# Retention attention in chunks of 64 tokens on quarters of TensorE's array, in a fused attention and feed-forward kernel

## The chip, the cores and the metric

The kernel runs on one core of a Trainium2 chip. The metric is the device time of one execution in microseconds (us). Before the change, three runs took 1265.42, 1265.68 and 1266.92 us; the median is 1265.68 us. The engines are named as the profile names them: PE is TensorE's multiplying, PEld its loading of weights (the stationary operand), DVE is VectorE, ACT is ScalarE, POOL is GpSimd and SP is SyncE, whose queue issues most of the DMAs.

## The reference

Two blocks follow each other. The first is a retention attention over 8 batches, 8 heads, 576 tokens and a head size of 64; the second is a gated feed-forward network on the 4608 tokens by 512 features that the first one gives.

```python
# q, k, v: (8, 8, 576, 64) float32
scores = q @ k.transpose(0, 1, 3, 2) / np.sqrt(64)
gamma = 1.0 - 2.0 ** (-5.0 - np.arange(8))
rel = pos[:, None] - pos[None, :]
Dmat = np.where(rel >= 0, gamma[:, None, None] ** rel, 0.0)
x = (scores * Dmat) @ v                  # then (B, H, S, D) -> (B*S, H*D)

xn = x / sqrt(mean(x * x, -1) + 1e-6) * rms_g
out = (silu(xn @ w_gate) * (xn @ w_val)) @ w_out     # 512 -> 1536 -> 512
```

There is no softmax, so the attention can be cut into chunks of tokens. Within a chunk the scores are taken directly, masked and multiplied by `v`. What comes from earlier chunks is a running 64x64 state per head (the sum of decayed `k` times `v`), which is multiplied by `q`. The decay is split into factors on `v`, on the state and on the output.

## The kernel before

**Jobs and slots.** The attention is cut into 32 jobs: one job is one batch and one pair of heads. The two heads of a pair lie on partitions 0 to 63 and 64 to 127 of `qT` and `kT`. The sequence of 576 tokens is cut into four chunks of 128 and a tail of 64. `slot(j)` issues the TensorE work of two neighbouring jobs: for job j the products `scores` (L242: 8 of 64 rows by 128 columns by 128, and 2 of 64x64 for the tail) and `states` (L252: 8 products with 128 rows and 64 columns); for job j-1 the products `values` (L292: masked scores times `v`, 8 with 128 rows, 64 columns and 128 moved elements, and 2 for the tail) and `carried` (L306: state times `q`, 4 products on the whole array, with the two heads' states on the diagonal of a 128x128 tile `sd`, whose other two quarters are zero). Every float32 product shows in the trace as two records, each with its own weight load.

**DVE and ACT around it.** `weigh(j)` multiplies all four full chunks' scores by the mask in one instruction of 128x1024 (L264), then the tail (L269), and then sums the states up in a chain of one copy (L272) and three steps (L274). ACT copies the sums into the diagonal of `sd` (L280). After `carried`, three DVE instructions of 128x192 (L315) write the attention's output into `x`. `following(j)` then transposes `q` and `k` of the next job on DVE (L212), scales `v` in place on ACT (L221, L222) and issues the loads of the job after that on SP's queue.

**Feed-forward.** The tokens go in 12 blocks u of 384. Blocks 0 and 1 use plain products (L470) while the weights are still being loaded and converted. From block 2 on, `up(u, m, g)` forms seven products x, y, z, x again, w, z again, w again (L413), each of eight records of 128x192, and ACT and DVE combine them between (L437, L420, L430). `down(u, s)` (L484) multiplies by `w_out`.

**Order.** The order of all instructions is written out by hand, and each engine does its own in that order. `SLOTS` puts the slots of the attention between the products of the feed-forward: behind `up` products 0, 2, 4 and 5 of one block, behind the first `down` of the next block, and behind products 1, 3 and 5 of the third. `scores` and `states` of a job go to three PSUM banks of their own (`s`). The other five banks are a pool, from which `values` takes two and each `up` takes four.

## Time and profile before

| | us |
|---|---|
| median of 3 runs | 1265.68 (1265.42 to 1266.92) |
| the profiled execution's own time | 1266.15 |
| its span, first to last instruction | 1264.4 |
| PE busy | 1217.4 |
| PEld busy | 924.2 |
| DVE busy | 547.6 |
| ACT busy | 280.3 |
| POOL busy | 43.0 |

The span is what the profile covers; 1.75 us of the execution lie around it. A PE record's duration covers its way through the array, so records overlap, and the pace of PE is read from the distance of their starts, not from their durations. The mean granted clock of TensorE was 0.984. In a row of the timeline stand the start and the duration in us, then engine, line, operation, out<-in and shape, the count of instructions (x) and in brackets the idle time before and who ended it.

### The profile page before, as it was taken

What the parts mean: (1) busy time and instruction counts of PE and PEld (TensorE: products, weight loads), DVE (VectorE), ACT (ScalarE), POOL (GpSimd) and SP (SyncE); (2) the same over time, 40 slices, a digit from 0 to 9 for tenths busy, and PEclk for the clock granted to TensorE, in tenths of its full rate; (3) what the DMA queues carried; (4) which work ended last, traced back from release to release, by engine and by line L of the source; (5) the groups of instructions that cost most, each with busy time, mean ns of one, the idle gap of its engine ahead of it and who ended that gap; (6) DMA issues with size and microseconds to landing.
All of it is one profiled execution on the core that took longest, in us unless ns stands there. A gap on an engine that the chain in (4) does not pass through costs nothing.

```text
span 1264.4 us, 16414 instructions
## 1 busy us (share of the span) xinstructions
PE 1217.4 (96%) x6792; PEld 924.2 (73%) x6792; DVE 547.6 (43%) x1056; ACT 280.3 (22%) x520; POOL 43.0 (3%) x44
## 2 busy tenths in 40 slices
PE   4599799999999999999999999999999999999998
PEld 3465455447976985976985995995995896795993
DVE  1789871015542652433552464343454443333240
ACT  3646541011221220111120221121221121120110
POOL 0000005130000000000000000000000000000000
PEclk8899799999999999999999999999999999999999
DMA  8579520022230322002122233002122200000000
GB/s 212 123 177 198 141 100 0 17 62 45 46 74 17 68 51 54 1 9 54 38 40 58 38 59 68 9 1 53 27 57 53 45 1 10 17 1 17 9 1 25
DMA packets 225307, 65.68 MB, mean 52 GB/s; under 512 B 212688, under 2 KB 212816, under 8 KB 225232
## 3 DMA queue, kind: packets, MB, share of 16 engines
q1 hardware_dynamic: 215872, 45.12, 17.3%
q10 hardware_dynamic: 9360, 19.51, 4.7%
q8 instruction: 53, 0.87, 0.3%
q14 instruction: 22, 0.18, 0.0%
HBM read 55.16 MB, written 9.44 MB: 51 GB/s over the span
## 4 chain that ended last, share of the span: by engine, by line
PE 88%; DVE 5%; ACT 3%; DMA 2%; issue 1%; SPq 1%; POOL 0%; DVEq 0%; ACTq 0%; POOLq 0%
PE out L484 29%; PE x L413 12%; PE w L413 12%; PE z L413 12%; PE y L413 6%; PE up L470 6%; PE s L242 3%; PE av L292 2%; PE av L306 2%; PE s L252 1%; DMA k<-in_k_dram 1%; ACT w_gate L548 1%; PE ms L360 1%; DVE w_gate L572 1%; DMA v<-in_v_dram 1%
## 5 line engine op out<-in xcount | busy, mean ns | idle before, releaser
L484 PE MATMUL out<-w_out,h 128*128 128x512 f32 x792 | 346.1, 594 | 0.0
L484 PEld LDWEIGHTS out<-w_out,h 128*128 128x128 f32 x792 | 149.1, 190 | 177.5 <-issue 175.1
L489 ACT COPY o_all<-out 128x512 f32<-128x512 f32 x36 | 21.1, 586 | 348.8 <-PE out L484 334.9
L420 DVE TENSOR_TENSOR u<-m,y 128x384 f32<-128x384 f32 x60 | 33.2, 554 | 149.9 <-PE y L413 141.8
L264 DVE TENSOR_TENSOR ret<-s,causal 128x1024 f32<-128x1024 f32 x32 | 39.2, 1224 | 121.8 <-PE av L292 69.3
L413 PE MATMUL x<-x,w_gate 128*128 128x192 f32 x480 | 88.9, 328 | 1.5 <-ACT m L437 1.5
L413 PE MATMUL x<-x,w_val 128*128 128x192 f32 x480 | 89.2, 329 | 0.0
L413 PE MATMUL w<-sums,w_gate 128*128 128x192 f32 x480 | 87.8, 326 | 0.0
L413 PE MATMUL w<-sums,w_val 128*128 128x192 f32 x480 | 87.8, 326 | 0.0
L413 PE MATMUL z<-x,w_gate 128*128 128x192 f32 x480 | 87.8, 326 | 0.0
L413 PE MATMUL z<-x,w_val 128*128 128x192 f32 x480 | 87.8, 326 | 0.0
L413 PEld LDWEIGHTS x<-x,w_gate 128*128 128x128 f32 x480 | 79.2, 190 | 7.1 <-issue 4.3
L413 PEld LDWEIGHTS x<-x,w_val 128*128 128x128 f32 x480 | 78.8, 190 | 1.4 <-ACT m L437 1.4
L413 PEld LDWEIGHTS w<-sums,w_gate 128*128 128x128 f32 x480 | 79.7, 190 | 0.0
L413 PEld LDWEIGHTS z<-x,w_val 128*128 128x128 f32 x480 | 79.7, 190 | 0.0
L413 PEld LDWEIGHTS z<-x,w_gate 128*128 128x128 f32 x480 | 79.7, 190 | 0.0
L413 PEld LDWEIGHTS w<-sums,w_val 128*128 128x128 f32 x480 | 79.7, 190 | 0.0
L280 ACT ACTIVATE sd<-sum,gc 64x256 f32<-64x256 f32 x64 | 32.3, 504 | 200.4 <-DVE sum L274 200.0
L470 PE MATMUL up<-x,w_gate 128*128 128x384 f32 x192 | 67.8, 515 | 1.5 <-ACT w_gate L548 0.8
L420 DVE TENSOR_TENSOR h<-u,w 128x384 f32<-128x384 f32 x60 | 33.3, 555 | 81.4 <-PE w L413 81.4
L432 ACT ACTIVATE h<-h 128x384 f32<-128x384 f32 x90 | 47.0, 523 | 88.6 <-DVE h L420 88.6
L382 DVE SCALAR_TENSOR_TENSOR x<-x,rms_g,rb 128x384 f32<-128x384 f32 x48 | 26.3, 608 | 89.1 <-PE rb L380 89.1
(98 smaller groups left out, 1345.7 us busy)
## 6 DMA issues: line engine op xcount, KB each, us to landing
out_dram<-o_all SPq DMA_DIRECT2D x36, 256.0 KB, 2.0
k<-in_k_dram SPq DMA_DIRECT2D x64, 128.0 KB, 2.8
v<-in_v_dram SPq DMA_DIRECT2D x64, 128.0 KB, 2.8
qraw<-in_q_dram SPq DMA_DIRECT2D x112, 72.0 KB, 2.4
kraw<-in_k_dram SPq DMA_DIRECT2D x112, 72.0 KB, 2.6
w_out<-in_moe_w_gate_dram ACTq DMA_DIRECT2D x6, 1024.0 KB, 6.6
w_out<-in_moe_w_val_dram ACTq DMA_DIRECT2D x3, 1024.0 KB, 5.9
w_gate<-in_moe_w_val_dram ACTq DMA_DIRECT2D x3, 1024.0 KB, 6.2
```

Of the source, the lines that this page charges most:

```text
L242: nc.tensor.matmul(s[:, e, ck] if c < NFULL else s[e * n : e * n + n, 2, :n], lhsT=d["kT"][r, ck], rhs=d["qT"][r, ck], start=True, stop=True,)
L264: nc.vector.tensor_tensor(out=ret.rearrange("p e (c k) -> p e c k", c=NFULL), in0=s[:, :2].rearrange("p e (c k) -> p e c k", c=NFULL), in1 ...
L280: nc.scalar.activation(out=sd[j % 2][r, :, r], in_=t[r], func=AF.Copy, scale=gc[r, hp : hp + 1])
L292: nc.tensor.matmul(av[blk][e * D : e * D + D, o : o + n], lhsT=d["v"][:, c, e] if c < NFULL else d["vt"][r], rhs=d["ret"][:, e, c * P : c ...
L306: nc.tensor.matmul(av[blk][:, o : o + n], lhsT=sd[j % 2][:, c - 1], rhs=d["qT"][:, c * P : c * P + n], start=False, stop=(c in (AC - 1, NC ...
L382: nc.vector.scalar_tensor_tensor(out=x[:, c], in0=x[:, c], scalar=rms_g[:, c : c + 1], in1=rb[:, :U], op0=ALU.mult, op1=ALU.mult,)
L413: nc.tensor.matmul(ps[:, i * HU : i * HU + HU], lhsT=w_up[m][:, 2 * blk + c, cut], rhs=t_of[u][blk][:, c], start=(start and i == c == 0), ...
L420: nc.vector.tensor_tensor(out=o, in0=a, in1=pairs_of(ps), op=ALU.add)
L432: nc.scalar.activation(out=o, in_=c, func=AF.Silu)
L470: nc.tensor.matmul(ps[:, :U], lhsT=w_up[m][:, 4 * half + c, i * P : i * P + P], rhs=x_of[u][:, c], start=(c == 0), stop=(c == NHP - 1),)
L484: nc.tensor.matmul(ps[:, :DM], lhsT=h_of[u][:, f, s * P : s * P + P], rhs=w_out[:, f], start=(f == 0), stop=(f == NF - 1),)
L489: nc.scalar.copy(out=o, in_=ps[:, :DM])
```

## The change

The chunk becomes 64 tokens: nine chunks (`NC`), numbered in pairs (`i, odd = divmod(c, 2)`). All attention products become 64x64x64, each on one quarter of the array: rows 0 to 63 or 64 to 127 by columns 0 to 63 or 64 to 127. `scores` takes rows by head and columns by the chunk's parity, `states` and `values` take rows by parity and columns by head, `carried` takes rows and columns by head, which are the two quarters on the diagonal. A tenth pair of scores repeats chunk 8, so that DVE has a full shape to read.

`sd` and its copies by ACT go; `carried` reads the sums directly, and the sums are kept in two buffers. The sum is a chain over eight chunks. The mask is one instruction for each head, which also multiplies by a constant. The state of chunk 7 finds no room in `s` and takes a bank `last` of the pool of five. The output is written by four instructions that step over every second chunk. `vt` (the tail of `v`) is loaded by one DMA instead of two and scaled by two instructions instead of one. Two small tables are no longer loaded, and another one is smaller.

In `slot`, `values` of the job before now comes ahead of `scores` and `states`. Behind the last product of `values`, GpSimd writes one element (`tick`) once that product is done, and the first product of `carried` waits for that write.

```diff
 def load_kv(j):
...
-        t = st[j]["vt"] = raw.tile([P, D], F32, tag="vt", name=f"vt_{j}", bufs=3)
-        for e in range(2):
-            nc.sync.dma_start(
-                out=t[e * TAIL : e * TAIL + TAIL], in_=v[b, 2 * hp + e, NFULL * P :]
-            )
+        t = st[j]["vt"] = raw.tile([L, 2, D], F32, tag="vt", name=f"vt_{j}", bufs=3)
+        nc.sync.dma_start(
+            out=t, in_=v[b, 2 * hp : 2 * hp + 2, NFULL * P :].rearrange("e p d -> p e d")
+        )
...
 def scale_v(j):
...
-            t = d["v"][:, :, e]
-            nc.scalar.activation(out=t, in_=t, func=AF.Copy, scale=gv[:, hp, e : e + 1])
-        nc.scalar.activation(out=d["vt"], in_=d["vt"], func=AF.Copy, scale=gt[:, hp : hp + 1])
+            for t in (d["v"][:, :, e], d["vt"][:, e]):
+                nc.scalar.activation(
+                    out=t, in_=t, func=AF.Copy, scale=gv[: t.shape[0], hp, e : e + 1]
+                )
+    def side(i):
+        return slice(i * L, i * L + L)
 def scores(j):
...
+        for c in range(NC + 1):
+            i, odd = divmod(c, 2)
+            c = min(c, NC - 1)
             for e in range(2):
                 nc.tensor.matmul(
+                    s[side(odd), e, i * L : i * L + L], lhsT=d["kT"][side(e), c * L : c * L + L],
+                    rhs=d["qT"][side(e), c * L : c * L + L], start=True, stop=True,
                 )
+    def state_of(d, c):
+        i, odd = divmod(c, 2)
+        if odd and SC + i * L == 512:
+            return d["last"][:, :L]
+        return d["s"][:, 1, SC + i * L : SC + i * L + L] if odd else d["s"][:, 2, i * L : i * L + L]
 def states(j):
...
+        d["last"] = bank(f"last_{j}")
+        for c in range(NC - 1):
+            i, odd = divmod(c, 2)
+            o = state_of(d, c)
+            for e in range(2):
+                nc.tensor.matmul(
+                    o[side(e)], lhsT=d["k"][side(odd), i, e],
+                    rhs=d["v"][side(odd), i, e], start=True, stop=True,
                 )
 def weigh(j):
...
+        ret = d["ret"] = att.tile([P, 2, NFULL + 1, L], F32, tag="ret", name=f"ret_{j}", bufs=1)
+        for e in range(2):
             nc.vector.scalar_tensor_tensor(
+                out=ret[:, e], in0=s[:, e, :SC].rearrange("p (c k) -> p c k", k=L),
+                scalar=float(_gamma(H)[2 * hp + e] ** -L),
+                in1=causal.unsqueeze(1).to_broadcast([P, NFULL + 1, L]),
+                op0=ALU.mult, op1=ALU.mult,
+            )
+        t = d["sum"] = att.tile([P, NC - 1, L], F32, tag="sum", name=f"sum_{j}")
+        for c in range(NC - 1):
+            part = state_of(d, c)
+            if c == 0:
+                nc.vector.tensor_copy(out=t[:, 0], in_=part)
+                continue
+            nc.vector.scalar_tensor_tensor(
+                out=t[:, c], in0=t[:, c - 1], scalar=gc[:, hp : hp + 1], in1=part,
                 op0=ALU.mult, op1=ALU.add,
             )
-        for e in range(2):
-            r = slice(e * D, e * D + D)
-            nc.scalar.activation(
-                out=sd[j % 2][r, :, r], in_=t[r], func=AF.Copy, scale=gc[r, hp : hp + 1]
-            )
+    def follow(a, b):
+        why = mybir.DependencyInfo(mybir.DependencyClass.Sync, mybir.DependencyReason.DATA)
+        tc.add_manual_dep(a.ins, b.ins.name, why, reason="rows of the array")
 def values(j):
...
+            i, odd = divmod(c, 2)
             for e in range(2):
+                mm = nc.tensor.matmul(
+                    av[odd][side(e), i * L : i * L + L],
+                    lhsT=d["v"][side(odd), i, e] if c < NC - 1 else d["vt"][:, e],
+                    rhs=d["ret"][side(odd), e, i],
+                    start=(c < 2), stop=False, skip_group_check=True,
+                )
+        d["valued"] = nc.gpsimd.memset(tick, 0.0)
+        follow(d["valued"], mm)
 def carried(j):
...
+            for e in range(2):
+                mm = nc.tensor.matmul(
+                    av[odd][side(e), i * L : i * L + L], lhsT=d["sum"][side(e), c - 1],
+                    rhs=d["qT"][side(e), c * L : c * L + L],
+                    start=False, stop=(c >= NC - 2), skip_group_check=True,
+                )
+                if c == 1 and e == 0:
+                    follow(mm, d["valued"])
...
+            for first in (c0 // L, c0 // L + 1):
+                i, odd = divmod(first, 2)
+                n = -(-(c1 // L - first) // 2)
                 nc.vector.tensor_tensor(
+                    out=x[:, first - c0 // L :: 2],
+                    in0=av[odd][:, i * L : (i + n) * L].rearrange("p (c k) -> p c k", k=L),
+                    in1=gq[:, hp].unsqueeze(1).to_broadcast([P, n, L]), op=ALU.mult,
                 )
 def slot(j, rest=True):
...
+        if rest and j > 0:
+            values(j - 1)
         if j < len(jobs):
             scores(j)
             states(j)
-        if rest and j > 0:
-            values(j - 1)
         if j < len(jobs):
             weigh(j)
         if rest and j > 0:
             carried(j - 1)
```

How the order on PE moves in one slot of the last third (the slot of job 31, between two `up` of block 9). Before, with L242 scores, L252 states, L292 values and L306 carried:

```order
L242 MATMUL s_5892<-qT_5792,kT_5794 128x128 x8
L242 MATMUL s_5892<-qT_5792,kT_5794 64x64 x2
...
L252 MATMUL s_5892<-v_5644,k_5641 64x64 x6
...
L292 MATMUL av_0_5911<-ret_5774,v_5444 64x128 x5
L292 MATMUL av_1_5912<-ret_5774,v_5444 64x128 [waits PE_49]
...
L306 MATMUL av_0_5911<-qT_5624,sd_97 128x128 x2
...
L413 MATMUL x_1_2_5941<-x_4862,w_val 128x192 [waits Activation_49]
...
L413 MATMUL z_1_2_5943<-x_4862,w_val 128x192 [waits DVE_49]
```

With the change, where L297 is values, L235 scores, L255 states, L316 carried and L430 the product of `up`:

```order
L297 MATMUL av_0_7165<-ret_7032,v_6633 64x64 [waits PE_49]
...
L297 MATMUL av_0_7165<-ret_7032,v_6633 64x64 x2
L297 MATMUL av_1_7166<-ret_7032,v_6633 64x64 x2
...
L235 MATMUL s_7186<-qT_7064,kT_7066 64x64 x20
...
L255 MATMUL s_7186<-v_6875,k_6872 64x64 x12
L255 MATMUL last_7207<-v_6875,k_6872 64x64 [waits Activation_49]
L316 MATMUL av_1_7166<-qT_6854,sum_7035 64x64 [waits Pool_49]
...
L316 MATMUL av_0_7165<-qT_6854,sum_7035 64x64 x2
...
L430 MATMUL x_1_2_7256<-x_5923,w_val 128x192 [waits DVE_49]
...
L430 MATMUL z_1_2_7258<-x_5923,w_val 128x192 [waits DVE_49]
```

`values` stands ahead of `scores`, `carried` waits for POOL, and what DVE has to finish ahead of the product z now comes from the bank `last` (in the change's program, z waits for the sum of chunk 7, the next w for the output's third instruction).

On DVE, behind the same products of `up`, before (L264 and L269 the masks, L272 and L274 the sum, L315 the output, here in the slot before, which has the transposes L212 too):

```order
L264 TENSOR_TENSOR ret_5774<-s_5743,causal 128x1024 [waits PE_49]
L269 TENSOR_TENSOR rett_5775<-s_5743,causal_t 128x64 [waits PE_49]
L272 COPY sum_5778<-s_5743 128x64
L274 SCALAR_TENSOR_TENSOR sum_5778<-sum_5778,gc,s_5743 128x64 [waits DVE_49] x3
L315 TENSOR_TENSOR x_4865<-av_0_5762,gq 128x192 [waits PE_49]
```

And with the change, in the slot of job 31 (L268 the masks, L278 and L280 the sum, L331 the output, L437 the first sum of `up`):

```order
L268 SCALAR_TENSOR_TENSOR ret_7224<-s_7186,causal 128x320 [waits PE_49]
L268 SCALAR_TENSOR_TENSOR ret_7224<-s_7186,causal 128x320
L278 COPY sum_7227<-s_7186 128x64
L280 SCALAR_TENSOR_TENSOR sum_7227<-sum_7227,gc,s_7186 128x64 [waits DVE_49] x6
L280 SCALAR_TENSOR_TENSOR sum_7227<-sum_7227,gc,last_7207 128x64 [waits DVE_49,PE_49]
L331 TENSOR_TENSOR x_5926<-av_0_7165,gq 128x2x64 [waits PE_49]
L331 TENSOR_TENSOR x_5926<-av_1_7166,gq 128x64
L331 TENSOR_TENSOR x_6851<-av_1_7166,gq 128x3x64
L331 TENSOR_TENSOR x_6851<-av_0_7165,gq 128x3x64
L437 TENSOR_TENSOR u_9_1_2_7261<-m_9_1_2_7260,y_1_2_7257 128x384 [waits PE_49,Activation_49]
```

One mask instruction of 1024 elements a row has become two of 320, three steps of the sum have become seven, and three output instructions four.

More of the change, by code (lines that the diff above doesn't have):

```diff
@@ L15 @@
 P = 128
+L = P // 2
 def _gamma(H):
@@ L619, in start @@
         make_identity(nc, ident)
-        for t in sd:
-            nc.gpsimd.memset(t, 0.0)
         nc.vector.memset(ones, 1.0)
```

88 lines of the change are left out of this document (22 added, 66 removed).

## The prediction

> **What bounds the kernel now.** I read the page first (busy times and the chain of waits), then the table of busy time by stage, then one slot in the timeline.
>
> ```profile
> span 1264.4 us, 16414 instructions
> PE 1217.4 (96%) x6792; PEld 924.2 (73%) x6792; DVE 547.6 (43%) x1056; ACT 280.3 (22%) x520; POOL 43.0 (3%) x44
> PE 88%; DVE 5%; ACT 3%; DMA 2%; issue 1%; SPq 1%; POOL 0%; DVEq 0%; ACTq 0%; POOLq 0%
> ```
>
> The chain that ended last runs over PE for 88% of the span. By stage (PE, PEld, DVE, ACT, POOL in this order), and, in the second fence, the mask instruction L264 alone, which runs once for each job:
>
> ```profile
> 0.00:137.30 137.30, 96.38 (x689) 67.60 (x689) 94.12 (x165) 73.54 (x113) 2.50 (x9) 0.88 0.73 176
> 290.60:1053.40 762.80, 761.31 (x4722) 620.89 (x4720) 338.83 (x698) 146.02 (x309) 5.96 (x7) 1.00 0.19 40
> ```
>
> ```profile
> 290.60:1053.40 762.80, 28.16 (x23) 1.00 0.19 40
> ```
>
> From 290.6 to 1053.4 us PE works for 761.3 of 762.8 us at full granted clock, and 23 of the 32 slots lie there. What the change does to PE in a slot counts there in full. In the first 137 us PE stands still for 41 us, and DVE and ACT, which convert the weights, share the chain. One slot of the long stage:
>
> ```profile
> 337.77 1.42 PE L242 MATMUL s<-qT,kT 64*128 64x128 f32 x20
> 339.12 0.69 PE L252 MATMUL s<-v,k 128*64 128x64 f32 x16
> 339.64 1.05 PE L292 MATMUL av<-ret,v 128*64 128x128 f32 x16
> 340.61 0.33 PE L292 MATMUL av<-rett,vt 64*64 64x64 f32 x4
> 340.88 1.10 PE L306 MATMUL av<-qT,sd 128*128 128x128 f32 x8
> 341.82 1.52 PE L413 MATMUL x<-x,w_gate 128*128 128x192 f32 x8
> 343.17 1.46 PE L413 MATMUL y<-sums,w_gate 128*128 128x192 f32 x8
> 344.47 1.46 PE L413 MATMUL z<-x,w_gate 128*128 128x192 f32 x8
> ```
>
> The slot lasts from 337.77 to 341.82, 4.05 us, for 64 records.
>
> **The change on PE.** It makes 140 records of 64 moved elements out of the 64: 36 for values, 40 for scores, 32 for states, 32 for carried. Whether that is shorter depends on how many run side by side. Before, the states' records have the same 64 elements and go on two halves of the array:
>
> ```profile
> 339.23 0.46 PE L252 MATMUL s<-v,k 128*64 128x64 f32 x10
> ```
>
> ```profile
> L252 PE MATMUL s<-v,k x512: 222/222/367, 20.2 to 1042.2; 128*64 128x64 f32 x171
> L292 PE MATMUL av<-rett,vt x128: 218/267/366, 31.4 to 1054.8; 64*64 64x64 f32 x128
> ```
>
> The first row is a narrow look: ten records, each 222 ns long (second row, median), within 0.46 us. The last starts 0.24 us after the first, which is four steps for five records of each half: 59 ns a step. One half gives a record every 59 ns, and the other half gives one in the same time. Two row halves run together as well: carried's eight records on the whole array, worth seven of 128 elements, take 0.94 us, 0.13 each, and at that price the scores' 16 records of 128 alone would take 2.1 us one after another, where all 20 take 1.35. A quarter of its own operands, its own columns of PSUM or its own bank should do the same, so I take 59 ns for a record of each quarter, all four at once. The fullest quarter has 10 records of values, 10 of scores, 8 of states and, since carried uses two quarters only, 16 of carried: 44 x 0.059 = 2.60 us. For the changes of the array's shape at both ends I take 0.15 us: the tail's four records hold PE from 340.61 to 340.88, 0.27 us, where two steps are 0.12. Sum 2.75 us instead of 4.05, **1.30 us less a slot, 23 x 1.30 = 29.9 us**. Bounds: no gain from quarters at all (below, first rival), and 2.60 us without any extra for the ends, 33 us.
>
> **The partial slots.** Job 8's scores and states stand alone before, and at the end values and carried of job 31:
>
> ```profile
> 256.69 1.42 PE L242 MATMUL s<-qT,kT 64*128 64x128 f32 x20
> ...
> 258.66 0.70 PE L484 MATMUL out<-w_out,h 128*128 128x512 f32 x1
> ```
>
> ```profile
> 1053.65 1.09 PE L292 MATMUL av<-ret,v 128*64 128x128 f32 x16
> ...
> 1055.88 0.65 PE L484 MATMUL out<-w_out,h 128*128 128x512 f32 x1
> ```
>
> The first takes 1.97 us, and would take 18 x 0.059 + 0.15 = 1.21: 0.8 less. The second takes 2.23, and would take 10 x 0.059, a wait of 0.5 (next part), 16 x 0.059 and 0.15: 2.18, nothing gained.
>
> **The wait by way of GpSimd.** Carried's first product waits for a write of POOL, which waits for the last of values; behind it on PE stand all of carried and the next `up`. What such a hop costs:
>
> ```profile
> 375.48 0.16 DVE L365 TENSOR_SCALAR r<-ms 128x3 f32<-128x3 f32 x1 [4.72 <-PE ms L360]
> 375.78 0.85 POOL L366 TENSOR_TENSOR r<-r,mhalf 128x3 f32<-128x3 f32 x1 [94.55 <-DVE r L365]
> 376.67 0.68 DVE L369 TENSOR_SCALAR diag<-ident,r 128x128 f32<-128x128 f32 x3 [1.03 <-POOL r L366]
> ```
>
> ```profile
> L728 POOL MEMSET const-float32-0.0<- 128x1 f32 x1 | 0.1, 99 | 0.2 <-issue 0.2
> ```
>
> 0.14 us to POOL, 0.10 for a small memset, 0.04 back: 0.28 us, after the last record's 0.22. So the write is seen 0.5 us after that record's start. Scores and states lie in between, 18 x 0.059 = 1.06 us, so it costs nothing as long as that cover is there; without it, 0.5 us a slot (12 us). POOL's queue holds seven other instructions in this stage (the stage row above), each of a block's normalisation behind its slots, and they come too late to delay it. At the two places in the first 137 us where values and carried follow each other directly, 0.5 us each may show; I count them there.
>
> **DVE and ACT.** The same slot:
>
> ```profile
> 340.73 1.23 DVE L264 TENSOR_TENSOR ret<-s,causal 128x1024 f32<-128x1024 f32 x1 [1.71 <-PE av L292]
> ...
> 342.00 0.22 DVE L272 COPY sum<-s 128x64 f32<-128x64 f32 x1
> 342.25 0.91 DVE L274 SCALAR_TENSOR_TENSOR sum<-sum,gc,s 128x64 f32<-128x64 f32 x3
> 343.08 0.88 DVE L315 TENSOR_TENSOR x<-av,gq 128x192 f32<-128x192 f32 x3
> 343.20 1.02 ACT L280 ACTIVATE sd<-sum,gc 64x256 f32<-64x256 f32 x2 [12.65 <-DVE sum L274]
> 343.88 0.77 DVE L212 STREAM_TRANSPOSE qT<-qraw 128x576 f32<-128x576 f32 x1
> ...
> 345.30 0.46 ACT L437 COPY m<-x 128x384 f32<-128x384 f32 x1
> 345.79 0.55 DVE L420 TENSOR_TENSOR u<-m,y 128x384 f32<-128x384 f32 x1 [0.49 <-ACT m L437]
> 345.81 1.57 PE L413 MATMUL x<-x,w_gate 128*128 128x192 f32 x8
> ```
>
> ```profile
> L382 DVE SCALAR_TENSOR_TENSOR x<-x,rms_g,rb 128x384 f32<-128x384 f32 x48 | 26.3, 608 | 89.1 <-PE rb L380 89.1
> L274 DVE SCALAR_TENSOR_TENSOR sum<-sum,gc,s 128x64 f32<-128x64 f32 x96 | 26.9, 281 | 3.4
> ```
>
> A mask of 320 lies between the last two rows: 281 + 256/320 x 327 = 543 ns. Two masks, the copy with its step to the chain (0.25) and seven steps of 0.30 make 1.05 + 0.25 + 2.1 = 3.4 us; four outputs about 0.97. That is 1.1 us more than from 340.73 to 343.96 before. In the slot's own time, with 0 at its first record: the state of chunk 6, on whose mark the masks wait in the change's program, starts at 1.6 and is through at 1.85; the sums end at 5.25. PE then wants product z at 2.75 + 1.35 + 1.30 = 5.40, with its weights loaded 0.16 earlier, and z waits for the last sum: **0.1 us late** in each of the 16 slots of this stage that an `up` follows (by the table of slots: one at its start, three or two in six of its blocks), +1.6 us (0 to 13, third rival). Next in line: outputs until 6.2, the two transposes until 7.6, two sums of `up` until 8.8; the second z product, which needs them, comes at 9.3. Covered by 0.5 us. ACT loses the two copies of 0.5 us and gains some 0.3 for the second tail. Its copy m no longer comes late for the second x product (345.81 instead of 344.47 + 1.30 = 345.77): 16 x 0.04, 0.6 us less.
>
> **The first 137 us.** Job 7's end shows who waits there:
>
> ```profile
> 131.98 1.01 ACT L280 ACTIVATE sd<-sum,gc 64x256 f32<-64x256 f32 x2
> 133.04 1.97 PE L306 MATMUL av<-qT,sd 128*128 128x128 f32 x8 [0.48 <-ACT sd L280]
> ```
>
> Eight slots bring DVE 8 x 1.1 = 9 us more work there and take 8 x 0.7 = 6 us off ACT; carried no longer waits for `sd`, each job's load list is one DMA shorter, and turning q and k of the next job needs banks that `last` now shares. I take +2, between -5 (ACT's share alone) and +9 (DVE's alone).
>
> **Sum.** -29.9 + 1.6 - 0.8 - 0.6 + 2 = -27.7 against this execution's own 1266.15: 1238.4. The median shown lies 0.5 below that execution, so I say **1238**; its own range is 1228 to 1250.
>
> **The rivals.**
>
> First, slower: PE hands out records no faster than it is seen to, two in 59 ns, and four quarters only share that pace. Then a slot is 140 x 0.0295 + 0.15 = 4.28 us, 0.23 more; 31 slots give +7, job 8 and the end +0.5, DVE in the first stage +2: 1275. It decides from 3.9 us for the 140 records, 28 ns each. For it: no row shows a longer run at a faster pace. Against it: both rows that I have are explained by each half's own 59 ns. Chance 0.14. The Trainium skill has a rule of this kind: "TensorE: Matmul & The Clock Gate" (Part 1, "Wait — 56ns, not 53.3ns?") says that starts of matmuls never come closer than about 25 ns however small they are; by it, an estimate, the slot takes 140 x 0.025 + 0.15 = 3.65 us and the kernel some 1258. The trace can't settle it: 0.24 us for nine distances is 27 ns on average.
>
> Second: records on different row halves that write the same PSUM bank go one after the other. Only carried has that; its 32 records then take 1.89 instead of 0.94 us, 23 x 0.94 = +22: 1260. Against it stands the tail at 340.61: its two products do just that, and four records of at least 218 ns fit in 0.33 us, so the last started 0.11 after the first, where one after the other would need 0.18. Chance 0.06. "TensorEngine Tiling (Array Packing)" of the Trainium skill ("Gotcha 1: PSUM Pressure") states that different row tiles can't use one bank at the same time; the trace disagrees in these four records.
>
> Third: DVE's masks begin as late as before, 1.1 us behind the states' end (340.73 after 339.64). Then the sums end at 6.15, z is 0.8 late in 16 slots, +13 instead of 1.6: 1250. For it: the row before names values, not states, as the releaser. Against: in the new order nothing stands between the states and their mark. Chance 0.10.
>
> Fourth: the gain is there and is lost to waits on banks or on POOL that I don't see, so that nothing remains within 0.2%. Chance 0.04.
>
> **Chances.** Forecast 0.62, rivals 0.14, 0.06, 0.10, 0.04; 0.04 for a loss of another kind, such as DVE in the first stage. No change means within 0.2%, about 2.5 us, which is what a measurement of this kernel can tell. Faster: 0.62 + 0.06 + 0.10 + 0.02 of the first rival at a slightly better pace, 0.80; same 0.05; slower 0.15. The range goes from 1228 to 1264, which takes in the second and third rival and leaves out the first.
>
> **What will show it.** Forecast: a slot of about 2.75 us with records of the four quarters starting within some 20 ns and then 59 ns apart; no PE idle before carried named after POOL; z at most 0.1 late. First rival: even starts of 25 to 30 ns. Second: carried at 1.9 us. Third: PE idle before z, named after DVE's sum. I am wrong if the slot is not below 3.5 us or if PE waits more than 0.5 us behind it.

## The result and the profile after

| | before | after |
|---|---|---|
| median of 4 runs, us | 1266.26 | 1228.47 (1227.20 to 1229.58) |
| the profiled execution's own time | 1266.15 | 1228.28 |
| its span | 1264.4 | 1226.5 |

The changed kernel takes 0.9702 of the time before (95% interval 0.9685 to 0.9718). It is 37.8 us faster; forecast were 27.7.

The page of the changed kernel (span, busy times, chain of waits):

```profile
span 1226.5 us, 21417 instructions
PE 1175.6 (96%) x9224; PEld 894.6 (73%) x9224; DVE 567.0 (46%) x1216; ACT 257.5 (21%) x488; POOL 45.2 (4%) x74
PE 87%; DVE 1%; ACT 0%; issue 0%; POOL 0%; ACTq 0%; DVEq 0%; POOLq 0%
```

The shares of this chain add up to 88%: it is followed back from the end only to 133.9 us, where the chain of the page before goes back to 0.7 us. So DVE's 5% then and 1% now, and ACT's 3% and 0%, can't be compared; they say nothing of the first 134 us. Behind that point PE has nearly all of the chain (87 of the 88%).

To see where the 37.9 us of the two profiled executions went, I cut both spans at the same two places of the program: the first slot of the long stage (that of job 9, "slot 9" below) and the last slot, which has only values and carried. Table of busy time by stage, before and then after (length of the stage, then PE, PEld, DVE, ACT, POOL):

```profile
0.00:291.07 291.07, 249.36 (x1140) 149.13 (x1140) 146.39 (x239) 108.73 (x162) 35.39 (x35) 0.93 0.44 112
291.07:1053.65 762.58, 761.09 (x4721) 620.92 (x4720) 339.04 (x698) 145.55 (x309) 5.96 (x7) 1.00 0.19 40
1053.65:1264.30 210.65, 206.98 (x933) 154.20 (x932) 62.18 (x119) 25.99 (x50) 1.70 (x2) 1.00 0.03 12
```

```profile
0.00:283.71 283.71, 239.48 (x1784) 140.94 (x1784) 152.29 (x283) 101.32 (x154) 35.40 (x41) 0.94 0.46 114
283.71:1015.40 731.69, 729.45 (x6469) 599.78 (x6468) 352.49 (x813) 130.18 (x285) 7.98 (x30) 1.00 0.20 42
1015.40:1226.40 211.00, 206.68 (x973) 153.93 (x972) 62.21 (x120) 25.99 (x50) 1.79 (x3) 1.00 0.03 12
```

The long stage is 30.9 us shorter (forecast 28.9). The part ahead of it is 7.4 us shorter, where the forecast had 1.2 us **more** (+2 and job 8's -0.8). The rest is unchanged (+0.35). So nearly all of the miss lies ahead of slot 9, and that is what the experiments had to explain.

One ordinary slot of the long stage, in the timeline (the slot that stood at 337.77 before):

```profile
328.55 0.69 PE L297 MATMUL av<-ret,v 64*64 64x64 f32 x32
...
329.12 0.23 PE L297 MATMUL av<-ret,vt 64*64 64x64 f32 x2
329.17 0.70 PE L235 MATMUL s<-qT,kT 64*64 64x64 f32 x36
...
329.83 0.09 POOL L305 MEMSET tick<- 1x1 f32 x1 [21.37 <-PE av L297]
...
330.18 1.14 PE L316 MATMUL av<-qT,sum 64*64 64x64 f32 x32
330.44 0.89 DVE L268 SCALAR_TENSOR_TENSOR ret<-s,causal 128x320 f32<-128x320 f32 x2 [0.64 <-PE s L255]
...
331.25 1.57 PE L430 MATMUL x<-x,w_gate 128*128 128x192 f32 x8
331.50 1.86 DVE L280 SCALAR_TENSOR_TENSOR sum<-sum,gc,s 128x64 f32<-128x64 f32 x6
...
333.47 0.28 DVE L280 SCALAR_TENSOR_TENSOR sum<-sum,gc,last 128x64 f32<-128x64 f32 x1
...
333.96 1.46 PE L430 MATMUL z<-x,w_gate 128*128 128x192 f32 x8
```

From 328.55 to 331.25 it lasts 2.70 us (forecast 2.75, before 4.05). The 32 records of carried go through two quarters in 1.14 us; less the last record's 0.23 that is 0.91 for 15 steps of each quarter, 61 ns a step. The masks begin 1.89 us after the slot's start (forecast 1.85). The sums end at 333.75, 5.20 after the start (forecast 5.25), z's weights start to load 0.16 ahead of 333.96, and z isn't late.

Who waited for ACT's copy `m`, before and after (total us of waiting, number of times), from the view of that tile:

```profile
  PEld x L413: 4.2, 15
```

```profile
  ACT sq L363: 6.2, 4
```

Before, 15 products stood still for ACT's `m`. After, none does.

### The profile page after: what moved, and what is told of

Same layout as the page of the kernel before. It is cut to its first block, busy times and chain, and to the rows that moved or that the text cites. A ratio compares the mean times of both kernels' runs of the same rounds, so it can differ in the third digit from the quotient of the medians.

```text
span 1226.5 us, 21417 instructions
## 1 busy us (share of the span) xinstructions
PE 1175.6 (96%) x9224; PEld 894.6 (73%) x9224; DVE 567.0 (46%) x1216; ACT 257.5 (21%) x488; POOL 45.2 (4%) x74
## 4 chain that ended last, share of the span: by engine, by line
PE 87%; DVE 1%; ACT 0%; issue 0%; POOL 0%; ACTq 0%; DVEq 0%; POOLq 0%
PE out L501 30%; PE x L430 13%; PE z L430 13%; PE w L430 13%; PE y L430 6%; PE up L487 6%; PE av L316 2%; PE av L297 1%; PE s L235 1%; PE s L255 1%; PE rb L397 1%; PE ms L377 0%; DVE x L399 0%; DVE w_val L597 0%; DVE sum L280 0%
## 5 line engine op out<-in xcount | busy, mean ns | idle before, releaser
L437 DVE TENSOR_TENSOR u<-m,y 128x384 f32<-128x384 f32 x60 | 32.7, 545 | 141.4 <-PE y L430 141.4
L430 PE MATMUL z<-x,w_gate 128*128 128x192 f32 x480 | 87.9, 326 | 2.2 <-DVE sum L280 2.2
L430 PE MATMUL x<-x,w_val 128*128 128x192 f32 x480 | 88.8, 328 | 0.0
L430 PE MATMUL x<-x,w_gate 128*128 128x192 f32 x480 | 88.5, 328 | 0.0
L430 PE MATMUL w<-sums,w_gate 128*128 128x192 f32 x480 | 87.8, 326 | 0.0
L430 PE MATMUL z<-x,w_val 128*128 128x192 f32 x480 | 87.8, 326 | 0.0
L430 PE MATMUL w<-sums,w_val 128*128 128x192 f32 x480 | 87.8, 326 | 0.0
L430 PEld LDWEIGHTS x<-x,w_gate 128*128 128x128 f32 x480 | 79.5, 190 | 4.8 <-issue 4.3
L430 PEld LDWEIGHTS z<-x,w_gate 128*128 128x128 f32 x480 | 79.6, 190 | 2.5 <-DVE sum L280 2.5
L430 PEld LDWEIGHTS w<-sums,w_val 128*128 128x128 f32 x480 | 79.7, 190 | 0.0
L430 PEld LDWEIGHTS w<-sums,w_gate 128*128 128x128 f32 x480 | 79.7, 190 | 0.0
L430 PEld LDWEIGHTS z<-x,w_val 128*128 128x128 f32 x480 | 79.6, 190 | 0.0
L430 PEld LDWEIGHTS x<-x,w_val 128*128 128x128 f32 x480 | 79.2, 190 | 0.6
L454 ACT COPY m<-x 128x384 f32<-128x384 f32 x60 | 28.7, 479 | 202.9 <-PE x L430 202.9
L437 DVE TENSOR_TENSOR h<-u,w 128x384 f32<-128x384 f32 x60 | 33.3, 554 | 76.4 <-PE w L430 76.4
L268 DVE SCALAR_TENSOR_TENSOR ret<-s,causal 128x320 f32<-128x320 f32 x64 | 28.4, 486 | 86.8 <-PE last L255 49.8
```

Source lines behind the costliest of these rows:

```text
L268: nc.vector.scalar_tensor_tensor(out=ret[:, e], in0=s[:, e, :SC].rearrange("p (c k) -> p c k", k=L), scalar=float(_gamma(H)[2 * hp + e] ** ...
L430: nc.tensor.matmul(ps[:, i * HU : i * HU + HU], lhsT=w_up[m][:, 2 * blk + c, cut], rhs=t_of[u][blk][:, c], start=(start and i == c == 0), ...
L437: nc.vector.tensor_tensor(out=o, in0=a, in1=pairs_of(ps), op=ALU.add)
L454: nc.scalar.copy(out=s1, in_=pairs_of(x_))
```

## The experiments

The first four ask two things. What paces the quarters: does each take its own work as it comes, so that only the fullest counts, or is something shared? And does the time ahead of slot 9 come from ACT, which no longer waits for the sums since the copies into `sd` are gone?

**1 and 2. Eight products more on one quarter.** Eight score products are issued a second time, in a row, behind all scores; in the one kernel on a quarter off the diagonal (which has 28 records and waits while carried runs), in the other on one of the diagonal, the fullest.

```diff
 def scores(j):
...
+        for c in (1, 3, 5, 7) * 2:        # the other kernel: (0, 2, 4, 6) * 2, and side(0)
+            nc.tensor.matmul(
+                s[side(1), 0, c // 2 * L : c // 2 * L + L], lhsT=d["kT"][side(0), c * L : c * L + L],
+                rhs=d["qT"][side(0), c * L : c * L + L], start=True, stop=True,
+            )
```

> The changed kernel with eight more products of 64x64x64 in each slot with scores (the scores of head 0 for chunks 1, 3, 5 and 7 taken twice more, to the same place), all on the quarter of rows 0 to 63 and columns 64 to 127. Theory A, each quarter works through its own queue and the slot lasts as long as its fullest quarter: that quarter goes from 28 to 44 records and the quarter of rows and columns 0 to 63 has 44 already, so nothing changes: within 2 us of the changed kernel's 1228.5, slot 2.70 us. Theory B, the four share one pace that is a little under half of before's: 16 records more at 2.6/140 = 19 ns each are 0.30 us a slot, 31 slots, +9 us.

> The same eight extra products, but of chunks 0, 2, 4 and 6, so that they fall on the quarter of rows and columns 0 to 63, which also has carried. Theory A: that quarter goes from 44 to 60 records, 16 x 58 ns = 0.93 us a slot; 22 slots between the products of the feed-forward's long stage, some 8 in the first stage that partly hide it: +21 to +29 us, about 1254, slot 3.64 us. Theory B: as with the other quarter, +9 us.

Off the diagonal: 1252.33 us (ratio to before 0.9895, 0.9880 to 0.9910), 23.9 more than the changed kernel. On the diagonal: 1253.33 us (0.9905, 0.9888 to 0.9921). The slot is 3.59 us in the one and 3.64 in the other: 0.89 and 0.93 us longer. It makes no difference which quarter gets the work. The kernel with the extra work off the diagonal:

```profile
334.36 0.92 PE L240 MATMUL s<-qT,kT 64*64 64x64 f32 x13
335.06 0.27 PE L260 MATMUL s<-v,k 64*64 64x64 f32 x1
335.12 0.22 PE L240 MATMUL s<-qT,kT 64*64 64x64 f32 x1
```

While the 16 extra records (L240) go through one quarter, 58 ns each, the states (L260), which use all four, don't start: three quarters stand idle for 0.7 us. A quarter doesn't run ahead on its own by more than a few records: the first state starts at 335.06, when three extra records are still to come (the next at 335.12). Beyond that, a product whose quarter is taken holds up everything that comes behind it in the program. So the first run refutes the rule that only the fullest quarter counts: by it, the extra work off the diagonal should have cost nothing.

**3. The same eight products, one at a time between the pairs of carried**, on a quarter that carried doesn't use (they write bank `last`). For this `carried` is issued ahead of `weigh`; the rest of PE's order is as it was.

```diff
 def carried(j, more=None):
...
                 if c == 1 and e == 0:
                     follow(mm, d["valued"])
+            if more is not None:
+                w = st[more]
+                nc.tensor.matmul(
+                    w["last"][side(0), c * L : c * L + L] if c < 8 else w["last"][side(0), 7 * L :],
+                    lhsT=w["kT"][side(1), c * L : c * L + L],
+                    rhs=w["qT"][side(1), c * L : c * L + L], start=True, stop=True,
+                )
```

> After the first two extra-product runs theory A as I put it has fallen: eight extra products on a quarter that had room cost as much as on the fullest one, when they stand in one block. Theory C in its place: PE hands products out in the order of the program, a product whose quarter is busy holds up all behind it, and so a slot lasts as long as the runs of products on one quarter make it. Here eight extra products (scores of head 1 taken again, to free columns of the bank that holds the last state) go to the quarter of rows 64 to 127 and columns 0 to 63, one after each pair of carried, where that quarter is idle. Theory C: they cost nothing, slot 2.70 us, 1228.5 within 2. If extra records cost time wherever they stand (theory B or one like it): 0.3 to 0.9 us a slot, +9 to +24.

1230.21 us (0.9725, 0.9710 to 0.9740), 1.7 more than the changed kernel, and a slot of 2.70 us as without them.

```profile
333.41 0.22 PE L325 MATMUL last<-qT,kT 64*64 64x64 f32 x1
333.42 0.27 PE L316 MATMUL av<-qT,sum 64*64 64x64 f32 x2
333.47 0.22 PE L325 MATMUL last<-qT,kT 64*64 64x64 f32 x1
333.47 0.27 PE L316 MATMUL av<-qT,sum 64*64 64x64 f32 x2
```

The two records of an L316 row start 0.05 us apart (0.27 less the 0.22 of one record). So at 333.47 the second of the first row, the L325 and the first of the next row start together, on three quarters, within about 10 ns, and the next three 0.06 us later. With the first two runs this gives the rule for this kernel: products are handed out in program order, each quarter takes a record of 64 every 58 ns, and besides a quarter's own work it counts whether neighbours in the program lie on different quarters.

What the profiled execution takes more (it is the longest of the four, 1233.66 us) doesn't lie in the slots: slot 9 begins 1.4 us later, and from there to slot 10 it takes 25.41 us instead of 23.73. PE stands still there for 2.24 us, as in the changed kernel, and behind it the granted clock is 0.57 from 294 to 298 us, where the changed kernel's execution shows 1.00. Experiment 8's execution has the same 25.41 (clock 0.78 and 0.79 from 290 to 298 us).

**4 and 5. ACT waits again, or only works again.** Two ACT instructions of 64x256 per job at the place where the copies into `sd` stood, writing to a tile that nobody reads; in the one kernel they read the sums and so wait for them, in the other they read a constant table.

```diff
 def weigh(j):
...
+        for e in range(2):
+            r = side(e)
+            nc.scalar.activation(
+                out=spill[r, e].rearrange("p (c k) -> p c k", k=L), in_=t[r, 4:], func=AF.Copy,
+                scale=gc[r, hp : hp + 1],
+            )          # the other kernel: in_ is the table gq
```

> The changed kernel with two copies by ScalarE per job put back at the place where the copies to the diagonal tile stood: 64x256 from the last four sums, to a tile that nobody reads. They wait for the end of VectorE's chain of sums, and ScalarE's later work of the slot queues behind them. Theory Q: the gain of 6 us in the first 137 us, which I had put at -2 (a loss of 2), came mostly from ScalarE no longer waiting for the sums ahead of copying the turned q and k of the next job. Then +5 to +9 us, and the slots of jobs 1 to 3 start some 3 to 8 us later than in the changed kernel (21.6, 31.3 and 40.4 us). Theory D: the gain came from fewer and smaller loads; then within 2 us of 1228.5. In the long stage ScalarE has room, so at most 2 us there.

> As the one before, two copies of the same shape per job at the same place, but from a constant table, so that ScalarE has the same work and waits for nobody. If waiting for the sums is what counts (theory Q): +1 to +3 us only. If the mere work of ScalarE counts, 8 jobs x 1.0 us on a chain that VectorE and ScalarE share: +5 to +8 us, the same as with the wait. If the loads count: no change within 2 us.

With the wait 1255.87 us (0.9926, 0.9912 to 0.9941), 27.4 more than the changed kernel; with the work alone 1229.73 (0.9718, 0.9703 to 0.9732), 1.3 more (the single runs of the two overlap). So ACT's 0.5 us instructions are nearly free, and waiting in its queue is not. The expectation of +5 to +9 for the wait, at most 2 of them in the long stage, was far too small: 25.2 of the profiled execution's us lie in the long stage (756.9 us instead of 731.7). The kernel with the wait, in the long stage, and its waits for `m`:

```profile
320.97 1.04 ACT L288 ACTIVATE spill<-sum,gc 64x256 f32<-64x256 f32 x2 [12.51 <-DVE sum L281]
...
323.32 0.45 ACT L461 COPY m<-x 128x384 f32<-128x384 f32 x1
...
323.83 1.57 PE L437 MATMUL x<-x,w_gate 128*128 128x192 f32 x8 [1.28 <-ACT m L461]
```

```profile
  PEld x L437: 22.9, 16
```

ACT stands 12.5 us in its queue for the last sum and comes to `m` 2.35 us after that, behind the copies and the scaling of `v`, and PE waits for `m` in each of the 16 places, 22.9 us in all by its weight loads. (In slot 9 the granted clock also fell to 0.60 and 0.55, from 296 to 304 us, behind the wait.) Slot 9 begins at 288.08, 4.4 later than in the changed kernel, where 7.4 had been gained. But the chain of sums is longer in the changed kernel than before, so this wait is larger than the one that the change took away; that one I asked of the kernel before.

**6. The kernel before, with its copies into `sd` done by GpSimd.** Nothing else changes: chunks of 128, the old order, the same sums.

```diff
-            nc.scalar.activation(
-                out=sd[j % 2][r, :, r], in_=t[r], func=AF.Copy, scale=gc[r, hp : hp + 1]
-            )
+            nc.gpsimd.tensor_scalar(
+                out=sd[j % 2][r, :, r], in0=t[r], scalar1=gc[r, hp : hp + 1], scalar2=None,
+                op0=ALU.mult,
+            )
```

> The kernel BEFORE, with one edit: the two copies of the sums into the diagonal of sd are done by GpSimd instead of ScalarE. Theory (a part of the change's gain in the first 137 us, about 4 us, and 0.6 us behind it, comes from ScalarE no longer standing in its queue until the chain of sums is done): slot 9 starts 3 to 5 us earlier than 291.07 and the whole time is 1261 to 1263 against 1265.8. Rival (that gain is PE's shorter slots alone): within 2 us of 1265.8. If GpSimd's copies are slow (over 1.5 us each), carried waits for them in both cases and the run says less; then the start of slots 0 to 3 decides, where the sums are long done.

1257.73 us (0.9935, 0.9919 to 0.9950): 8.2 us of the old kernel go away with a changed engine name, more than either theory had. By stage:

```profile
0.00:286.46 286.46, 247.12 (x1140) 147.38 (x1140) 146.83 (x239) 99.55 (x145) 55.98 (x53) 0.94 0.45 114
286.46:1045.29 758.83, 758.83 (x4721) 621.36 (x4720) 336.35 (x698) 124.58 (x263) 48.49 (x53) 1.00 0.19 40
```

4.6 us ahead of slot 9 and 3.75 in the long stage, where I had put 0.6. Not all of the 4.6 need be the wait itself: 1.35 of them lie in the 32 products behind job 7's part, which take 13.20 us in the kernel before and 11.84 here (12.58 in the changed kernel), with a granted clock of 0.50 until about 144 us there and 137 us here. Why 0.6 was too little stands in the trace of before, in slot 9 and in the slot at 428.36:

```profile
298.12 1.02 ACT L280 ACTIVATE sd<-sum,gc 64x256 f32<-64x256 f32 x2 [6.96 <-DVE sum L274]
300.23 0.46 ACT L437 COPY m<-x 128x384 f32<-128x384 f32 x1
...
300.74 1.57 PE L413 MATMUL x<-x,w_gate 128*128 128x192 f32 x8 [1.49 <-ACT m L437]
```

```profile
433.77 1.46 PE L413 MATMUL y<-sums,w_val 128*128 128x192 f32 x8
...
434.91 1.33 PEld L413 LDWEIGHTS z<-x,w_val 128*128 128x128 f32 x8
435.07 1.46 PE L413 MATMUL z<-x,w_val 128*128 128x192 f32 x8
...
436.40 1.27 PEld L413 LDWEIGHTS x<-x,w_val 128*128 128x128 f32 x8 [0.17 <-ACT m L437]
436.40 1.57 PE L413 MATMUL x<-x,w_val 128*128 128x192 f32 x8
437.81 1.46 PE L413 MATMUL w<-sums,w_val 128*128 128x192 f32 x8
```

Undisturbed, a product follows the one before by 1.30 us (433.77 to 435.07). The late one comes after 1.33, which I had counted; but then its own eight records take 1.41 instead of 1.30 until the next product starts, since its weight loads had not run ahead (the first one starts with it at 436.40, where z's starts 0.16 ahead of z). So a wait of 0.03 us cost 0.14, and in slot 9 it cost 1.76 (24.16 us to slot 10's start, 22.40 here). From one such slot to the next, the kernel before takes 22.54 us and this one 22.40.

**7. Values behind scores and states**, as in the order before, so that nothing lies between values and the write that carried waits for.

```diff
 def slot(j, rest=True):
...
-        if rest and j > 0:
-            values(j - 1)
         if j < len(jobs):
             scores(j)
             states(j)
+        if rest and j > 0:
+            values(j - 1)
```

> The changed kernel with values issued behind scores and states, as before the change, so that carried follows values directly and the wait for GpSimd's write has no cover. In the changed kernel the write ends 0.43 us after the start of values' last record and is seen 0.05 later, with 0.61 us to spare. Without cover: the slot lasts 2.70 + 0.43 = 3.1 us, 0.4 x 22 slots in the long stage and up to 8 in the first: +9 to +13, 1237 to 1242. If the wait does not matter or another one covers it: within 2 us of 1228.5.

1240.57 us (0.9804, 0.9789 to 0.9819), 12.1 more than the changed kernel; a slot of 3.20 us. One slot:

```profile
309.29 0.29 PE L297 MATMUL av<-ret,vt 64*64 64x64 f32 x4
309.71 0.09 POOL L305 MEMSET tick<- 1x1 f32 x1 [23.70 <-PE av L297]
...
309.85 1.15 PE L316 MATMUL av<-qT,sum 64*64 64x64 f32 x32 [0.27 <-POOL tick L305]
```

The way over GpSimd, uncovered, is 0.5 us a slot, as the prediction priced it.

**8. A long write on GpSimd**: `tick` is a tile of 128x512, all of which is written.

> GpSimd's write after values is a memset of 128x512 elements instead of one element; nothing else changes. In the changed kernel's slots the way over GpSimd (0.35 us to POOL, 0.09 us memset, 0.05 us back) ends 0.61 us before PE comes to carried. A memset of 128x512 should take 0.5 to 0.6 us, so 0.45 us of the 0.61 are used up. Theory (the wait is fully covered, with that much to spare): slot stays 2.70 us, whole time within 2 us of 1228.5, PE never idle ahead of carried in the long stage. Rival (the cover is thinner than I read it, since PE's queue must see the write some time before carried can start): slot grows by up to 0.4 us, 22 slots, up to +9 us, 1237.

1230.12 us (0.9716, 0.9698 to 0.9733), 1.65 more than the changed kernel; in the profiled execution 1.68 us more lie between slot 9 and slot 10, with the lower clock named under experiment 3. The write takes 0.52 us instead of 0.09, and all slots of the long stage but one stay at 2.70; that one, where GpSimd began later than elsewhere, is 2.94. So 0.44 us more on this way were covered. Its row in the slot that stretched:

```profile
330.11 0.23 PE L297 MATMUL av<-ret,vt 64*64 64x64 f32 x2
...
330.83 0.52 POOL L305 MEMSET tick<- 128x512 f32 x1 [20.93 <-PE av L297]
```

**9. DVE late**: one DVE instruction of 128x512 more per job, ahead of the chain of sums, into a tile that nobody reads.

```diff
 def weigh(j):
...
+        nc.vector.tensor_tensor(
+            out=spill, in0=s[:, 1, :].rearrange("p (h k) -> p h k", h=NHP),
+            in1=ident.unsqueeze(1).to_broadcast([P, NHP, P]), op=ALU.mult,
+        )
```

> The changed kernel with one dead DVE instruction more in each job (128x512, from the scores' banks to a tile that nobody reads), between the masks and the chain of sums: about 0.65 us. No work of the kernel is left out. It prices my third rival (DVE late by 0.8 us makes product z wait). Theory: in the ordinary slots the sums end 0.2 us ahead of z, so z waits about 0.45 us in 16 slots of the long stage (+7), and the first stage takes up to +5 because DVE shares its chain: 1235 to 1241. Rival (DVE has slack of its own of the order of 0.5 us that I do not see): 1228 to 1231.

1242.51 us (0.9820, 0.9804 to 0.9835), 14.0 more than the changed kernel and just above the range of the theory. Slot 9 begins at 288.24, 4.5 later; from there to the last slot it is 9.1 us longer. In the slot at 334.21:

```profile
336.91 0.68 DVE L275 TENSOR_TENSOR spill<-s,ident 128x512 f32<-128x512 f32 x1
...
339.73 0.28 DVE L285 SCALAR_TENSOR_TENSOR sum<-sum,gc,last 128x64 f32<-128x64 f32 x1
...
340.06 1.57 PE L435 MATMUL z<-x,w_gate 128*128 128x192 f32 x8 [0.28 <-DVE sum L285]
```

z starts 5.85 us after the slot's start instead of 5.41. Together with 0.11 us in the product behind it, as in the old kernel's late x, an ordinary stretch from slot to slot takes 0.55 us more (21.65 instead of 21.10). DVE's chain of sums is next in line behind PE, with next to no slack: in the changed kernel the sums end at 333.75, 0.05 us ahead of z's first weight load, and 0.05 is also what lies between the two where z waits (340.01 and 340.06).

**10. Loads as before**: the tail of `v` comes by two DMAs again.

```diff
-        nc.sync.dma_start(
-            out=t, in_=v[b, 2 * hp : 2 * hp + 2, NFULL * P :].rearrange("e p d -> p e d")
-        )
+        for e in range(2):
+            nc.sync.dma_start(out=t[:, e], in_=v[b, 2 * hp + e, NFULL * P :])
```

> The changed kernel with the tail of v loaded by two DMAs again, as before the change. Theory Q (ScalarE's waiting made the first stage's gain): 0 to +1.5 us. Theory D (the shorter list of loads made it): +3 to +6.

1229.39 us (0.9714, 0.9697 to 0.9731), the same as the changed kernel within the intervals, and slot 9 begins at 282.69, no later than in it: the loads of the tail explain nothing ahead of slot 9. The smaller tables were not put back, so their share isn't tested.

**11. A version that follows from 1 to 3.** From job 4 on, chunks 0 to 2 of each head go to the quarter on the diagonal and chunks 3 to 8 to the one off it (for values, scores and states), and the products are issued in turn, one of the diagonal and one beside it, so that carried runs next to scores and states and the four quarters have nearly equal work. `k` and `v` are loaded by more DMAs, to the halves of the partitions that this asks for. Its core:

```diff
+    def spot(e, c):
+        return (e, c) if c < BW else (1 - e, c - BW)          # BW = 3
...
+        off += [(score, n, c) for c in A] + [(state, n, c) for c in A if c < NC - 1]
+        diag += [(score, n, c) for c in B] + [(state, n, c) for c in B]
+        cut = len(diag) + 1
+        if o:
+            diag += [None] + [(carry, o, c) for c in range(1, NC)]
+        for i in range(max(len(off), len(diag))):
+            for x in (diag, off):
...
```

> Chunks placed anew from job 4 on: chunks 0 to 2 of a head on the quarter of its own rows and columns, chunks 3 to 8 on the others, so that every quarter has 17 products of a slot (before: 22, 21, 14 and 13), and the products issued so that the quarters come in turn, carried beside the scores and states of chunks 3 to 8. k and v are loaded by four DMAs each. By theory C with 58 ns a record the slot takes 34 x 0.058 + 0.15 = 2.1 us, and 2.2 to 2.3 if carried waits for GpSimd's write: 0.4 to 0.55 us less in 22 slots, 9 to 12 us. VectorE's masks are 384 wide instead of 320 and its outputs two or three instructions instead of four; PE comes 0.5 us earlier to the products that need its sums, which may take 0.2 us in 16 slots back: 1217 to 1223. If the slot is set by the count of records alone (140, now 136): no gain, 1227 to 1230.

1222.68 us (0.9659, 0.9643 to 0.9675), 5.8 less than the changed kernel and the best of all. The slot is 2.30 us, 0.40 shorter; 23 such slots make 9.2 us, of which 6.9 are left in the long stage, and 1.75 are lost ahead of slot 9, which is within the scatter of that start (282.69 us in experiment 10, 285.10 in experiment 3). The slot fell together with the fullest quarter's work, 44 to 34 records, and with the order, so this run doesn't part the two. What bounds it now:

```profile
309.65 0.34 PE L248 MATMUL s<-qT,kT 64*64 64x64 f32 x6
309.68 0.09 POOL L307 MEMSET tick<- 1x1 f32 x1 [23.10 <-PE av L262]
309.82 0.27 PE L269 MATMUL av<-qT,sum 64*64 64x64 f32 x2
```

```profile
  PEld z L555: 3.5, 15
```

Carried starts 0.05 us behind the end of GpSimd's write in every slot of the long stage: the cover is used up. And the second z waits 15 times for DVE's `u` (second fence, the view of that tile).

## Why the prediction was right, and where it was not

**The slot: right, with a reason that was too simple.** 1.30 us less a slot, 29.9 in all, were forecast. Between the kernel with `sd` on GpSimd and the changed one, neither of which waits for `m`, an ordinary stretch from slot to slot goes from 22.40 us (331.26 less 308.86, the two slots' starts) to 21.10, 1.30 less, 29.9 for 23 slots. The slot itself is 1.35 shorter; 0.05 go back in the x behind it, whose eight records take 1.41 us (331.25 to 332.66) instead of 1.35. The step "the fullest quarter's 44 records set the slot" gave the right number by luck of the order: values, scores and states are spread evenly over four quarters and carried follows alone, which also makes 44 steps. Experiments 1 and 2 show that the count of the fullest quarter alone isn't the rule; the order counts.

**First rival (a shared pace): refuted.** It decided from 3.9 us; 140 records go through in 2.70, 19 ns each on average, and three start within 10 ns in experiment 3. By that row the trace does not agree with the 25 ns floor between starts in the Trainium skill's "TensorE: Matmul & The Clock Gate" (Part 1, "Wait — 56ns, not 53.3ns?"): it holds here for each quarter at most, not between quarters. The prediction's "the trace can't settle it" took an average for the distance: in the trace of before the records on two halves already start in pairs, 0.007 us apart (scores at 337.769 and 337.776, states at 339.346 and 339.353), with 0.05 us to the next pair of states.

**Second rival (one bank from two row halves): refuted.** Carried took 1.14 us with its last record's flight, not 1.9. The Trainium skill's "TensorEngine Tiling (Array Packing)" ("Gotcha 1: PSUM Pressure") states that different row tiles can't use one bank at the same time; these 32 records do so in pairs, at 61 ns a step against 58 elsewhere.

**Third rival (masks late): refuted, its price about right.** The masks begin where the forecast put them. Experiment 9 bears on what it would have cost: 0.68 us of delay made 9.1 us in the long stage, so 1.1 us, an estimate, would have made more than the 13 that I gave it (0.42 us more in each of 16 slots are another 7).

**Fourth rival (nothing left): refuted** by the result itself.

**The wait by way of GpSimd: right.** 0.28 us of hop behind the record's 0.22 were forecast; experiment 7 shows 0.5 us a slot without cover, and experiment 8 that 0.44 us more fit under scores and states. In the changed kernel PE's weight loads wait for it only at three places:

```profile
  PEld av L316: 1.3, 3
```

**z late: near in sum by luck, wrong in place.** Forecast were 0.1 us in 16 slots, +1.6; measured are 2.6, all in one slot. In ordinary slots z isn't late: DVE's masks take 486 ns each instead of the 543 estimated, as the page's group shows.

```profile
L268 DVE SCALAR_TENSOR_TENSOR ret<-s,causal 128x320 f32<-128x320 f32 x64 | 28.4, 486 | 86.8 <-PE last L255 49.8
```

In slot 9 it is 2.5 us late, which by the prediction's own signs (PE idle before z, named after DVE's sum, and more than 0.5 us behind the slot) is the third rival's mark in one slot out of 16. It is late there because the block's own sums (L410) stand ahead of the masks on DVE:

```profile
287.82 0.56 DVE L410 TENSOR_TENSOR sums<-x,sums 128x384 f32<-128x384 f32 x1
...
291.64 0.46 PEld L430 LDWEIGHTS z<-x,w_gate 128*128 128x128 f32 x3 [2.53 <-DVE sum L280]
```

**The copies into `sd`: the step that failed.** The prediction gave ACT's release 0.6 us in the long stage and, ahead of it, put everything together at +2 between "ACT's share alone" (-5) and "DVE's alone" (+9). Experiment 6 prices the release, wait and work together: 3.75 us in the long stage and up to 4.6 ahead of it. In the long stage I read only the start of the late product and not the product behind it, and I left out slot 9; the group of waits for `m` (4.2 us in 15 waits, quoted above) had about the right size for the long stage from the start. So the long stage is -29.9 for the slots, -3.75 for `m`, +2.6 for z in slot 9 (23.73 us to the next slot's start instead of 21.10): -31.0, where 30.9 were measured.

Ahead of slot 9, 7.4 us were gained instead of 1.2 lost. Up to 4.6 are the release of ACT (experiment 6, with the clock's part in it), and job 8's slot gave 0.76 (1.97 to 1.21 us), as forecast. The other 2.0 aren't measured one by one. PE's shorter slots and DVE's longer work both count there: 0.89 us more of PE in each of nine slots moved slot 9 by 3.7 us (experiment 1), and 0.68 us more of DVE in each of the first stage's eight jobs by 4.5 (experiment 9). DVE's extra work was also less than the 9 us forecast: its busy time ahead of slot 9 went from 146.39 to 152.29. What the 2.0 us consist of isn't settled by the runs; slot 9's start moves by about 1 us between kernels that differ only in the loads or in `tick` (282.69 and 283.02 against 283.71), and it is known for one execution of each kernel only. One new wait stands there, in the slot of job 6: the state of chunk 7 waits for the bank `last`, which the feed-forward still holds.

```profile
102.85 0.37 PE L255 MATMUL last<-v,k 64*64 64x64 f32 x2 [3.75 <-ACT h L495]
```

**The sum.** 1238 was forecast, with 1228 to 1250 as its own range; 1228.5 lies 0.5 us inside its edge. Of the 10.2 us that were missed in the profiled executions (37.9 less 27.7), 8.6 lie ahead of slot 9 and 2.0 in the long stage, 0.4 went the other way at the end. The release of ACT, which the sum priced at 0.6 and a guess, is the largest part of both; that the range held in spite of it is luck.

## What to carry to other kernels

When a change takes an instruction off an in-order engine, price what stood queued behind it, not its duration: two copies of 0.5 us cost 1.3 us as work alone (the second kernel of experiments 4 and 5), and 8.2 went away with two that also waited (experiment 6). Start that price with the group of all waits for the tile that comes late, since a product that starts late by 0.03 us also loses its weight prefetch and costs 0.14. When products go to quarters of TensorE's array, order them so that neighbours lie on different quarters; a run of products on one quarter holds up the other three.

## What the hardware showed that was not expected

- Work on quarters is handed out in program order and, but for a lead of some three records, held up at the first product whose quarter is taken (experiments 1 to 3: 0.89 us for eight products in a row, nothing for the same eight spread out).
- Which wait a small engine adds isn't quite constant: in the changed kernel GpSimd's write starts 0.35 us behind the start of the last record of values in 21 of the 23 full slots of the long stage and in the last one, 0.29 in slot 9, and 0.71 in the slot at 328.55 (329.12 to 329.83, quoted above). The same slot is the slow one in experiments 7, 8 and 11, where the wait shows on PE (3.53 instead of 3.20 us, 2.94 instead of 2.70, 2.66 instead of 2.30). No instruction of GpSimd stood ahead of it; why it is that slot stays open.
- The same wait of PE in slot 9, 2.24 us, is followed by a lower granted clock in some executions and not in others: 1.00 from 290 to 298 us in the changed kernel, 0.78 and 0.79 in experiment 8, which made 1.68 us more until slot 10. What decides it isn't shown.
